# K'V of two units in four 64x64 quarters, summed in two banks that one row of matmuls claims

## The chip, the cores and the metric

One core of a Trainium2 chip runs the whole program. The metric is the device time of one execution in microseconds (us); lower is better. The kernel before takes 1583.36 us (median of three runs, 1583.11 to 1583.88).

## The reference

```python
# 8 batches, 8 heads, 576 tokens, 64 wide; q, k, v float32
kv  = np.einsum('bhsd,bhse->bhde', k, v)            # K'V: 64 x 64 for each head
out = np.einsum('bhsd,bhde->bhse', q, kv)
rms = np.sqrt(np.mean(out * out, axis=-1, keepdims=True) + 1e-06)
x   = out / rms * g_norm                            # then (4608, 512), heads side by side
h   = x @ w_in                                      # 512 -> 2048
g   = s * np.maximum(h, 0) ** 2 + b
x   = g @ w_out                                     # 2048 -> 512
h   = x @ w_in2
out = (h * np.cos(h)) @ w_out2                      # the second layer, same sizes
```

The change touches the first line alone: K'V of each head, a sum over 576 tokens.

## The kernel before

The program has two parts. The first (up to some 360 us) does attention and 48 steps of the first layer, 3 token blocks of 512 by 16 slices of the hidden width. A step has four groups of hidden-layer matmuls (`mm_h`, L877 to L879, three matmuls in each), which sum into PSUM bank h0 or h2; ScalarE (L891) and, from step 12 on, VectorE (L898) read that bank; then four groups of second-layer matmuls (`mm_o`, L926 for the first block's steps 0 to 11, in plain float32, and L930 after that), which sum into other banks (a0 to a3). The rest of the program, with the second layer, reuses weights and products in a Strassen-like scheme (L1084, L1215 and others) and is not touched.

Attention is spread over the first part. A *unit* is two heads. The first token block has its K'V from `kv_first` (L689, K and V as 9 rows on 128 partitions, one head on each half). For every later batch two units at a time are done as one *row*, one operation on TensorE: first `mm_x` (L787) multiplies q' of two units by their K'V into the halves xa and xb of banks h1 and h3, in 64x64 quarters; then `kv_pair` (L712) makes K'V of the next two units. There are 14 such rows; the first holds K'V alone. `kv_pair` reads K and V as 96 partitions by 6 rows, four tiles for two units (three slots kv_raw and the slot raw), multiplies 96x64 pieces in two column halves, 6 passes x 2 heads x 2 units = 24 matmuls, and sums both units in one bank, h0 or h2, side by side. ScalarE copies each unit's K'V to kvf (L718, 128x64, two in a row). Also in h0 or h2: four transposes a unit (L822) some us behind the row, read by ScalarE (L854 or L861) and for early blocks by VectorE (L856). GpSimd's queue (POOL, called SUM in the code) loads K and V from the third block on (L660), SP's queue before; the loads wait until the row before has read the tiles. The same POOL queue stores pieces of the first layer's weights (L614, L617).

The order of all this is not written by hand. `Plan` takes operations with an engine, a cost in us, a due time and the tiles that they read and write, plays the program on a model of the engines, and picks at each point the ready operation with the earliest due time; a search over shifted due times keeps orders in which the modelled TensorE idles least. An operation that needs PSUM banks starts, in the model, when all of them are free. `START` is when each engine is first free in the model, `AFTER` and `SLACK` are the delay behind an operation and a factor on its cost. The order found is the order on each engine; on the chip each instruction waits for its own inputs and for its own bank.

```python
    SLACK = {"PE": 1.0, "DVE": 1.14, "ACT": 1.14, "POOL": 1.0}
    AFTER = {"PE": 0.2, "DVE": 0.13, "ACT": 0.14, "POOL": 0.13}
    ACC, HB0, HB1, HB2, HB3 = slots("a", 4), ["h0"], ["h1"], ["h2"], ["h3"]
```

## Time and profile before

| | |
|---|---|
| median of three runs | 1583.36 us |
| the profiled execution | 1583.36 us, its span 1581.6 us |
| TensorE matmuls busy | 1566.9 us, 99% |
| TensorE weight loads busy | 1462.7 us, 92% |
| VectorE, ScalarE busy | 76%, 72% |
| share of the chain that ended last on TensorE | 96% |
| L712 (K'V of the rows) | 672 instructions from 69.6 to 289.3 us |

The span is what the trace covers of the profiled execution; some 1.8 us lie around it. PE is TensorE's matmuls, PEld its weight loads, which run beside matmuls, DVE is VectorE, ACT ScalarE, POOL GpSimd. A float32 matmul stands in the trace as two instructions. The start of a weight load is the sharper mark: the ends of matmuls are modelled. "Idle before" is time in which an engine stood still, with what ended it.

### The profile page before, as it was taken

How to read it: one execution, taken by the hardware profiler on the slowest of the kernel's cores; microseconds unless marked ns; L12 is line 12 of the kernel's file. 1: busy time of each engine (PE TensorE's matmuls, PEld its weight loads, DVE VectorE, ACT ScalarE, POOL GpSimd, SP SyncE). 2: the span in 40 equal slices, each digit the busy share in tenths (PEclk: the TensorE clock that was granted, in tenths of full speed). 3: DMA queues.
4: the chain of work that ended last, by engine and by line, in shares of the span. 5: the costliest groups of instructions: out<-in, count | busy, mean ns of one | idle time of the engine just before them, and what ended most of it. 6: DMA issues, size and time to landing. Idle time of an engine off the chain costs nothing.

```text
span 1581.6 us, 30681 instructions
## 1 busy us (share of the span) xinstructions
PE 1566.9 (99%) x11200; PEld 1462.7 (92%) x11200; DVE 1208.5 (76%) x2335; ACT 1142.4 (72%) x2088; POOL 54.3 (3%) x90
## 2 busy tenths in 40 slices
PE   8999999999999999999999999999999999999998
PEld 7667888888999999999999999999999999999998
DVE  5888776687667667657778888888888888888776
ACT  5875654456667767657888888887887888888773
POOL 0012322000000000000000000000000000000000
PEclk9999999999999999999999999999999999999999
DMA  9856888859889988868987888978978878978857
GB/s 322 244 121 167 243 225 223 244 175 308 305 254 296 304 263 274 304 228 293 345 251 257 298 254 263 314 252 262 306 253 263 307 252 264 308 254 259 270 186 238
DMA packets 261814, 413.09 MB, mean 261 GB/s; under 512 B 88608, under 2 KB 169504, under 8 KB 261664
## 3 DMA queue, kind: packets, MB, share of 16 engines
q1 hardware_dynamic: 255072, 389.57, 76.9%
q0 software_dynamic: 6016, 20.45, 4.7%
q8 instruction: 89, 1.46, 0.4%
q10 hardware_dynamic: 576, 1.11, 0.2%
q14 instruction: 61, 0.50, 0.1%
HBM read 327.16 MB, written 83.89 MB: 260 GB/s over the span
## 4 chain that ended last, share of the span: by engine, by line
PE 96%; DMA 2%; ACT 1%; DVE 0%; issue 0%; SPq 0%; POOL 0%; DVEq 0%; POOLq 0%
PE banks L1084 37%; PE banks L1215 22%; PE banks L978 13%; PE banks L930 6%; PE banks L1222 4%; PE banks L877 3%; PE banks L878 3%; PE banks L926 3%; PE banks L879 3%; PE banks L787 1%; PE banks L712 1%; PE banks L822 1%; DMA q_raw<-in_q_dram 1%; DMA wi<-w2n_d 1%; PE banks L1378 0%; PE banks L689 0%
## 5 line engine op out<-in xcount | busy, mean ns | idle before, releaser
L1084 PE MATMUL banks<-shared,wi 128*128 128x384 f32 x2232 | 461.7, 337 | 1.0 <-ACT g L1097 1.0
L1084 PEld LDWEIGHTS banks<-shared,wi 128*128 128x128 f32 x2232 | 389.6, 188 | 4.2 <-ACT g L1097 1.3
L1215 PE MATMUL banks<-wi,fs 128*128 128x256 f32 x2250 | 290.2, 282 | 1.5 <-DMA wi<-w2n_d 0.9
L1215 PEld LDWEIGHTS banks<-wi,fs 128*128 128x128 f32 x2250 | 284.9, 190 | 2.0 <-DMA wi<-w2n_d 1.1
L978 PE MATMUL banks<-wi,wo 128*128 128x256 f32 (+1 forms) x984 | 210.5, 337 | 0.0
L978 PEld LDWEIGHTS banks<-wi,wo 128*128 128x128 f32 x984 | 161.5, 188 | 18.4
L1097 ACT ACTIVATE t<-banks 128x384 f32<-128x384 f32 x218 | 106.6, 489 | 99.2 <-PE banks L1084 74.4
L1133 DVE TENSOR_TENSOR fs<-fu,fs 128x384 fp32r<-128x384 f32 x240 | 129.6, 555 | 25.5 <-ACT fs L1132 24.0
L1132 ACT CAST fs<-fu 128x384 fp32r<-128x384 f32 x240 | 120.1, 507 | 17.8 <-PE banks L1215 12.1
L1084 PE MATMUL banks<-late,wi 128*128 128x384 f32 x552 | 125.3, 337 | 0.1
L1084 PE MATMUL banks<-g,wi 128*128 128x384 f32 x504 | 113.0, 338 | 0.0
L930 PE MATMUL banks<-g,wo 128*128 128x512 f32 x432 | 109.3, 396 | 0.0
L1170 ACT ACTIVATE wi<-wi 128x768 f32<-128x768 f32 x96 | 80.9, 842 | 27.1 <-DVE wi L1106 26.7
L1084 PEld LDWEIGHTS banks<-late,wi 128*128 128x128 f32 x552 | 97.1, 188 | 1.1 <-DVE c L497 0.5
L1176 DVE CUSTOM_DVE_ANT_0 wi<-wi,wi 128x768 f32<-128x768 f32 x96 | 91.2, 954 | 8.3 <-ACT wi L1174 8.2
L930 PEld LDWEIGHTS banks<-g,wo 128*128 128x128 f32 x432 | 79.3, 188 | 16.1
L1084 PEld LDWEIGHTS banks<-g,wi 128*128 128x128 f32 x504 | 87.3, 188 | 0.4 <-ACT t L1097 0.3
L1215 PE MATMUL banks<-wi,raw 128*128 128x256 f32 x612 | 84.0, 282 | 1.0 <-DMA wi<-w2n_d 1.0
L877 PE MATMUL banks<-shared,wi 128*128 128x512 f32 x192 | 81.7, 426 | 1.3 <-ACT shared L854 0.8
L1215 PEld LDWEIGHTS banks<-wi,raw 128*128 128x128 f32 x612 | 80.7, 189 | 1.3 <-DMA wi<-w2n_d 1.3
L1178 ACT ACTIVATE wi<-wi 128x768 f32<-128x768 f32 x96 | 80.5, 839 | 1.0 <-DVE wi L1176 0.9
L1172 ACT ACTIVATE wi<-wi 128x768 f32<-128x768 f32 x96 | 80.5, 843 | 0.1
(194 smaller groups left out, 2740.7 us busy)
## 6 DMA issues: line engine op xcount, KB each, us to landing
wi<-w2i_d SPq DMA_DIRECT2D x144, 512.0 KB, 4.7
wi<-w1i_d SPq DMA_DIRECT2D x96, 512.0 KB, 5.2
wi<-w2s_d SPq DMA_DIRECT2D x96, 512.0 KB, 4.5
wi<-w2n_d SPq DMA_DIRECT2D x40, 512.0 KB, 3.9
wi<-w2n_d SPq DMA_DIRECT2D x64, 256.0 KB, 4.0
late<-x_d SPq DMA_DIRECT2D x36, 384.0 KB, 6.2
wi<-in_moe_w_in_dram SPq DMA_DIRECT2D x24, 512.0 KB, 8.2
w2i_d<-t SPq DMA_DIRECT2D x48, 256.0 KB, 5.2
```

Of the source, the lines that this page charges most:

```text
L877: nc.tensor.matmul(h.t, wh, hi, start=(c == 0), stop=False)
L930: nc.tensor.matmul(o.t, a[:, sl], b, start=(first and z == 0), stop=(last and z == 2))
L978: nc.tensor.matmul(dst, x[:, sl], y[:, src], start=(first and z == i == 0), stop=(last and z == 2), skip_group_check=a >= 4)
L1084: nc.tensor.matmul(o.t[:, 0:HT], a, b, start=(first and c == z == 0), stop=(c == 1 and z == 2), skip_group_check=not first)
L1097: op("ACT", 0.38, by - 40, lambda: nc.scalar.activation(dst(), o.t[:, 0:HT], func), p=[s], r=[o])
L1132: op("ACT", 0.42, by, lambda: nc.scalar.copy(x.t[:, 0], src()), w=[x], r=[ref], after=after)
L1133: op("DVE", 0.47, by + 0.4, lambda: nc.vector.tensor_tensor(out=x.t[:, 1], in0=src(), in1=f32(x.t[:, 0]), op=ALU.subtract), w=[x], r=[ref])
L1170: op("ACT", 0.75, at, lambda u=u, x=x: nc.scalar.activation(u.t, x.t, AF.Identity, scale=1.0 / TWO_PI, bias=0.25), w=[u], r=[x])
L1172: op("ACT", 0.75, at + 0.5, lambda u=u, v=v: nc.scalar.activation(v.t, u.t, AF.Identity, bias=MAGIC), w=[v], r=[u])
L1176: op("DVE", 0.88, at + 2, lambda u=u, v=v: nc.vector._custom_dve(TENSOR_ADD_SAT, out=u.t, in0=u.t, in1=v.t, s0=0.5 - 1.7e-7, s1=-0.5 + 1.7 ...
L1178: op("ACT", 0.75, at + 3, lambda u=u: nc.scalar.activation(u.t, u.t, AF.Sin, scale=TWO_PI), w=[u])
L1215: nc.tensor.matmul(dst, x.t[:, a, sl], w.t[:, at, b, :], stop=(last and z == 2), start=(first and z == 0 and (m == 0 or (m == 2 and opens) ...
```

## The change

K and V of two units are loaded as 9 rows of 64 numbers on all 128 partitions, two tiles in place of four. Each load fills one half of the partitions of one tile with two heads: the lower half gets the first head of the first unit and the second head of the second, the upper half the other two, so that the heads are crossed over the halves. There are still four loads a row. Each of the 9 passes has four matmuls of 64x64, one for each pair of a partition half and a column half: 36 matmuls in place of 24. The first unit sums in bank h0, the second in h2. The row names both banks as a claim: while it is ready within 3 us and has no banks yet, the planner holds back TensorE operations that are due later and want one of them. Besides, the costs that the planner is told of the row, of the first units' products and of the plain float32 matmuls change, and so do the times at which TensorE and ScalarE are taken to start.

```diff
-    START = {"PE": 1.4, "DVE": 1.0, "ACT": 2.9, "POOL": 4.2, "SP": 0.8, "SUM": 4.2, "AQ": 0.8}
+    START = {"PE": 2.4, "DVE": 1.0, "ACT": 3.5, "POOL": 4.2, "SP": 0.8, "SUM": 4.2, "AQ": 0.8}
+    CLAIM = 3.0
...
                 base = max(engines[e], lanes[e][0]) if e in lanes else engines[e]
+                claims = [o for o in ops if o.claim and ready_at[o.n] < base + self.CLAIM]
+                if claims:
+                    c = min(claims, key=lambda o: due[o.n])
+                    ops = [o for o in ops if o is c or due[o.n] < due[c.n] or not any(
+                        slot[i] is None and c.claim.intersection(slots) for i, slots in o.placed)]
...
-    KV_RAW, Q_RAW = [*slots("kv_raw", 3), "raw"], slots("q_raw", 2)
+    KV_RAW, Q_RAW = slots("kv_raw", 2), slots("q_raw", 2)
...
-    def kv_load(queue, t, src, b, h0):
+    def kv_load(queue, t, src, b, h0, half):
+        heads = src[b, h0 + 1:h0 + 3] if half else src[b, h0:h0 + 4:3]
         queue.dma_start(
-            out=t.t[0:KP, 0:2 * R * D].rearrange("p (h r d) -> p h r d", h=2, r=R),
-            in_=src[b, h0:h0 + 2].rearrange("h (p r) d -> p h r d", r=R))
+            out=t.t[half * D:(half + 1) * D, :].rearrange("p (g n) -> p g n", g=2),
+            in_=heads.rearrange("g (p r) d -> p g (r d)", r=R0))
...
-        ps, loaded = pref(HB2 + HB0), []
-        for hp in hps:
-            pair = [sref(KV_RAW, F32, (2 * R * D,)) for i in range(2)]
+        ps, pair = [pref(HB0), pref(HB2)], [sref([KV_RAW[i]], F32, (2 * S,)) for i in range(2)]
+        for t, src in zip(pair, (k, v)):
             eng, queue = ("SP", nc.sync) if j < 2 else ("SUM", nc.gpsimd)
-            in_turn["kv"] = [op(eng, 0.95, by - 9, lambda t=t, src=src, hp=hp: kv_load(queue, t, src, b, 2 * hp), w=[t],
-                                after=after, behind=in_turn.get("kv", ())) for t, src in zip(pair, (k, v))]
-            loaded.append(pair)
+            in_turn["kv"] = [op(eng, 0.95, by - 9, lambda t=t, src=src, half=half: kv_load(queue, t, src, b, 2 * hps[0], half),
+                                p=[t], after=after, behind=in_turn.get("kv", ())) for half in range(2)]
...
         def mm():
-            for n, (k_t, v_t) in enumerate(loaded):
-                for r in range(R):
-                    for h in range(2):
-                        nc.tensor.matmul(ps.t[h * D:(h + 1) * D, n * D:(n + 1) * D], rows(k_t, h, r), rows(v_t, h, r),
-                                         start=(r == 0), stop=(r == R - 1))
+            for r in range(R0):
+                for h in range(2):
+                    for n in range(2):
+                        half = h if n == 0 else 1 - h
+                        k_r, v_r = (t.t[half * D:(half + 1) * D, n * S + r * D:n * S + (r + 1) * D] for t in pair)
+                        nc.tensor.matmul(ps[n].t[h * D:(h + 1) * D, 0:D], k_r, v_r, start=(r == 0), stop=(r == R0 - 1))
...
         return op("PE", cost, by, lambda: [x[0]() for x in parts], w=[y for x in parts for y in x[1]],
-                  r=[y for x in parts for y in x[2]])
+                  r=[y for x in parts for y in x[2]], claim=[*HB0, *HB2])
...
-        op("PE", 0.45, by - 3, transpose_x, w=[xT], r=[xn])
+        op("PE", 0.38, by - 3, transpose_x, w=[xT], r=[xn])
...
-        x_ops.append(op("PE", 0.65, by - 8, mm, w=w, r=r))
+        x_ops.append(op("PE", 1.04, by - 8, mm, w=w, r=r))
...
-            row(0.85, by - 13, [kv[:3]])
+            row(1.25, by - 13, [kv[:3]])
...
-        x_ops.append(row(1.25 + (0.7 if kv else 0), by - 8, [*parts, kv and kv[:3]]))
+        x_ops.append(row(1.1 + (1.2 if kv else 0), by - 8, [*parts, kv and kv[:3]]))
...
-            done = op("PE", 0.87 if native else 0.69, by + step * m, lambda m=m, o=acc[m]: mm(m, o), w=[acc[m]],
+            done = op("PE", 0.91 if native else 0.69, by + step * m, lambda m=m, o=acc[m]: mm(m, o), w=[acc[m]],
...
-        op("ACT", 0.3, -99, lambda: nc.scalar.activation(
+        op("ACT", 1.4, -99, lambda: nc.scalar.activation(
```

## Rows read from the trace of the kernel before

**Rows 1.** The page: busy time of each engine, and the chain that ended last.

```profile
PE 1566.9 (99%) x11200; PEld 1462.7 (92%) x11200; DVE 1208.5 (76%) x2335; ACT 1142.4 (72%) x2088; POOL 54.3 (3%) x90
...
PE 96%; DMA 2%; ACT 1%; DVE 0%; issue 0%; SPq 0%; POOL 0%; DVEq 0%; POOLq 0%
```

**Rows 2.** Stretches: length, busy PE, PEld, DVE, ACT, POOL, granted clock, DMA share, GB/s.

```profile
0.00:20.00 20.00, 17.57 (x312) 16.52 (x314) 7.65 (x16) 8.66 (x18) 2.99 (x10) 1.00 0.85 288
20.00:40.00 20.00, 16.62 (x133) 11.92 (x129) 15.66 (x38) 13.47 (x26) 0.00 (x0) 1.00 1.07 354
...
180.00:240.00 60.00, 59.55 (x672) 49.58 (x672) 49.68 (x105) 31.33 (x66) 20.54 (x32) 1.00 0.85 227
```

**Rows 3.** Waits of TensorE's matmuls over the whole span: total us, times, longest.

```profile
PE banks L1378 <- POOL ident masks.py:199: 2.4, 1, 2.4
PE banks L1215 <- DMA wi<-w2n_d: 2.0, 2, 1.0
...
PE banks L787 <- DVE qT L771: 0.5, 1, 0.5
```

**Rows 4.** Timeline of weight loads, 87.9 to 91.0: the second row (start, us, count last).

```profile
87.91 1.02 PEld L787 LDWEIGHTS banks<-kvf,qT 64*64 64x64 f32 x64 [0.75 <-issue]
89.00 0.78 PEld L712 LDWEIGHTS banks<-kv_raw,kv_raw 96*64 96x64 f32 x24
89.69 0.79 PEld L712 LDWEIGHTS banks<-raw,kv_raw 96*64 96x64 f32 x24
90.55 0.19 PEld L877 LDWEIGHTS banks<-shared,wi 128*128 128x128 f32 x1
```

**Rows 5.** Line L712 over the span, one unit of two: count, ns, first and last start.

```profile
L712 PEld LDWEIGHTS banks<-raw,kv_raw x336: 138/138/138, 70.3 to 289.3; 96*64 96x64 f32 x168
```

**Rows 6.** Timeline of weight loads: kv_first, and what follows it on the same tile shape.

```profile
14.40 1.13 PEld L689 LDWEIGHTS banks<-wo,wo 64*64 64x64 f32 x36
15.45 1.02 PEld L747 LDWEIGHTS banks<-ident,wi 64*64 64x64 f32 x32
```

**Rows 7.** Stretches of 0.2 us: weight loads of L787, then of L712, that touch them.

```profile
88.30:88.50 0.20, 0.20 (x23) 1.00 0.00 0
...
89.30:89.50 0.20, 0.20 (x12) 1.00 0.00 0
```

**Rows 8.** Timeline of matmuls around the first row.

```profile
69.32 0.40 PE L879 MATMUL banks<-shared,wi 128*128 128x512 f32 x1
69.64 0.92 PE L712 MATMUL banks<-kv_raw,kv_raw 96*64 96x64 f32 x24
...
71.19 0.50 PE L877 MATMUL banks<-shared,wi 128*128 128x512 f32 x1
```

**Rows 9.** Timeline: the two readers of a hidden-layer sum, and what they waited for.

```profile
109.70 0.60 ACT L891 ACTIVATE t<-banks 128x512 f32<-128x512 f32 x1 [1.51 <-PE banks L879]
...
110.33 0.75 DVE L898 SCALAR_TENSOR_TENSOR t<-t,small,banks 128x512 f32<-128x512 f32 x1 [1.08 <-ACT t L891]
```

**Rows 10.** Timeline of ScalarE: copies of K'V behind the second row, the last behind the fourth.

```profile
90.67 0.33 ACT L718 COPY kvf<-banks 128x64 f32<-128x64 f32 x2 [0.44 <-PE banks L712]
...
118.41 0.21 ACT L718 COPY kvf<-banks 128x64 f32<-128x64 f32 x1
```

**Rows 11.** Last loads of two rows, their median landing, and the matmuls that use them.

```profile
92.16 0.64 POOL L660 DMA_DIRECT2D raw<-in_v_dram  x1
...
105.88 0.65 POOL L660 DMA_DIRECT2D raw<-in_v_dram  x1
...
raw<-in_v_dram POOLq DMA_DIRECT2D x12, 288.0 KB, 6.3
...
102.53 0.92 PE L712 MATMUL banks<-kv_raw,kv_raw 96*64 96x64 f32 x24
...
115.01 0.92 PE L712 MATMUL banks<-kv_raw,kv_raw 96*64 96x64 f32 x24
...
116.56 0.50 PE L877 MATMUL banks<-shared,wi 128*128 128x512 f32 x1
```

More of the change, by code (lines that the diff above doesn't have):

```diff
@@ L94, in __init__, with op @@
         self.parts = {}
-    def op(self, eng, cost, due, fn, w=(), p=(), r=(), keep=(), after=(), behind=(), lag=0.0):
+    def op(self, eng, cost, due, fn, w=(), p=(), r=(), keep=(), after=(), behind=(), lag=0.0, claim=()):
         o = Op()
+        o.claim = set(claim)
         o.eng, o.cost, o.due, o.fn, o.lag, o.refs = eng, cost, due, fn, lag, list(dict.fromkeys([*w, *p, *r, *keep]))
@@ L310, in fused_kernel @@
     NF1 = NP1 - NU
-    KP = 96
-    R = S // KP
     NQ, R0 = TB // D, S // D
@@ L408, in fused_kernel @@
     LATE = slots("late", 7)
-    EARLY = {*KV_RAW[:3], *Q_RAW, *KV_F, *QT, *AT}
+    EARLY = {*KV_RAW, *Q_RAW, *KV_F, *QT, *AT}
     RING, PLACES, X_RAW = WI[:5], slots("s", 11), LATE[:4]
@@ L695, in kv_pair @@
     def kv_pair(j, b, hps, by, after):
-        ps, loaded = pref(HB2 + HB0), []
-        for hp in hps:
-            pair = [sref(KV_RAW, F32, (2 * R * D,)) for i in range(2)]
+        ps, pair = [pref(HB0), pref(HB2)], [sref([KV_RAW[i]], F32, (2 * S,)) for i in range(2)]
+        for t, src in zip(pair, (k, v)):
             eng, queue = ("SP", nc.sync) if j < 2 else ("SUM", nc.gpsimd)
-            in_turn["kv"] = [op(eng, 0.95, by - 9, lambda t=t, src=src, hp=hp: kv_load(queue, t, src, b, 2 * hp), w=[t],
-                                after=after, behind=in_turn.get("kv", ())) for t, src in zip(pair, (k, v))]
-            loaded.append(pair)
-        def rows(t, h, r):
-            return t.t[0:KP, 0:2 * R * D].rearrange("p (h r d) -> p h r d", h=2, r=R)[:, h, r, :]
-        def mm():
-            for n, (k_t, v_t) in enumerate(loaded):
-                for r in range(R):
-                    for h in range(2):
-                        nc.tensor.matmul(ps.t[h * D:(h + 1) * D, n * D:(n + 1) * D], rows(k_t, h, r), rows(v_t, h, r),
-                                         start=(r == 0), stop=(r == R - 1))
+            in_turn["kv"] = [op(eng, 0.95, by - 9, lambda t=t, src=src, half=half: kv_load(queue, t, src, b, 2 * hps[0], half),
+                                p=[t], after=after, behind=in_turn.get("kv", ())) for half in range(2)]
+        def mm():
+            for r in range(R0):
[4 more added lines that the diff above has]
+                        nc.tensor.matmul(ps[n].t[h * D:(h + 1) * D, 0:D], k_r, v_r, start=(r == 0), stop=(r == R0 - 1))
         def copy():
@@ L717, in copy @@
                 tf = kv_f[b % 2, hp]
-                op("ACT", 0.21, by - 3, lambda n=n, tf=tf: nc.scalar.copy(tf.t, ps.t[:, n * D:(n + 1) * D]), w=[tf], r=[ps])
-        return mm, [ps], [x for pair in loaded for x in pair], copy
+                op("ACT", 0.21, by - 3, lambda n=n, tf=tf: nc.scalar.copy(tf.t, ps[n].t[:, 0:D]), w=[tf], r=[ps[n]])
+        return mm, ps, pair, copy
     xs = {}
```

## The prediction

> **What bounds the kernel now.** I began with the page. TensorE is busy for 99% of the span, and 96% of the chain that ended last is TensorE [rows 1]. A change pays only if it takes time from TensorE's own stream, and it costs if it makes TensorE wait. Next, the stretches: the rows that the change touches run from 69.6 to 289.3 us (the first and last L712 starts [rows 5, 8]). The worst of the four stretches of 60 us from 60 to 300 has TensorE busy for 59.55 of 60, VectorE for 49.68 and ScalarE for 31.33, at a granted clock of 1.00, the higher of its two levels (2.4 GHz) [rows 2]. The list of TensorE's waits agrees: in that stretch only the 0.5 us for qT is worth a name [rows 3]. So this stage is a gapless stream of matmuls, and each microsecond cut from it arrives at the end, if no gap opens.
>
> **How fast a small matmul is.** Each matmul of this kind stands in the trace as two instructions: a row of K'V has 24 in the code and 48 in the trace, 14 rows make 672, half of them on the second unit [rows 4, 5]. In kv_first, 36 weight loads on two 64x64 tiles take from 14.40 to 15.45 us, where instructions of the same tile shape follow: 18 couples in 1.05 us, 58.3 ns a couple [rows 6]. L712 (96 rows, two column halves) works in couples too: the second unit starts 0.69 us behind the first, 12 couples at 57.5 ns; all 24 are 1.40 us, and 1.55 stand there (89.00 to 90.55) [rows 4]. The 0.15 left over is the change to the shape that follows (128x128). L787, the product with q' on the four 64x64 quarters, issues 64 in 1.09 us (87.91 to 89.00): 16 sets of four at 58.3 ns are 0.93, and again some 0.15 for the change, here to 96 rows [rows 4]. The counts in flight show it too: 23 loads touch a 0.2 us window of L787, 12 one of L712 [rows 7]. So a set takes 58 ns however many tiles are in it, and four quarters do twice the work of two halves.
>
> **Part 1, the quarters.** A row now takes 9 x 2 x 2 = 36 matmuls, 72 instructions, in place of 48. On four quarters they are 18 sets: 18 x 58.3 ns = 1.05, and 0.15 for the change of shape behind them, 1.20 us against 1.55: 0.35 less, in 14 rows 4.9 us. In 13 rows (all but the first, by the code of attn_pair) L787 stands ahead, now of the same 64x64 shape, so the 0.15 between the two goes as well (as between L689 and L747 [rows 6]): 1.95 us. **Together 6.85 us** of TensorE's stream. Bounds: if the sums that stay open over nine passes, or the order (row half changes before column half), kept only two tiles in flight, the row would be 36 x 58.3 ns = 2.10 + 0.15, 0.70 longer than now. I take four in flight: L787 has the same shape, the same two row halves into two banks, and L689 keeps a sum open over nine passes at the common 58.3 ns [rows 4, 6].
>
> **Part 2, two banks claimed.** This is the cost. Before, a row sums into one of the banks h0, h2; the other could hold a hidden-layer sum, even one half done: at 69.64 us the row cuts into a run of L877 to L879, whose last three follow it, as in 7 of the 14 rows [rows 8]. Now both must be empty when the row's K'V starts, and both stay taken until ScalarE has copied them. (a) Before the row: a hidden sum is read by ScalarE from 109.70, as soon as its last matmul is done, to 110.30, and by VectorE from 110.33 to 111.08 [rows 9], so its bank is free 1.4 us later. Two things cover that: the second-layer matmuls (L926 or L930, four a step, 0.69 us each in the planner's costs), and L787 itself, 1.09 us, which uses other banks and runs ahead of K'V in the same row. I price it at nothing; uncovered it would be 1.4 - 1.09 = 0.33 us in a row, and up to 0.7 more if the reader is queued behind one other ScalarE or VectorE operation (0.60 to 0.75 [rows 9]). (b) Behind the row: the first copy starts 0.12 us after the next matmul would (90.67 against 90.55), the two end 0.33 later, at 91.00 [rows 4, 10]. A hidden-layer matmul put right behind the row would wait 0.33 to 0.45 us; second-layer matmuls put there hide it. Where ScalarE has other work first, a copy comes later (one at 118.41, 1.85 us behind the row [rows 10]), but that holds back only the one who needs that bank. The planner is told of the claim, and its model charges the copy (0.2 + 0.21 x 1.14 + 0.14 = 0.58 us), so it will mostly put second-layer work there. As the new order can't be read from this trace, I take one row in four paying 0.45: 14 / 4 x 0.45 = **1.6 us lost**. Bounds: nothing, and in each row 0.45 (6.3 us).
>
> **Part 3, loads and buffers.** Four loads a row as before, 288 KB each, 0.64 us of GpSimd each [rows 11]; POOL's w1i stores stay queued behind the same number. 128 pieces of 2304 bytes replace 192 of 1536. Buffers come free with the row's last matmul, as before. The tightest row: last load issued at 105.88, median landing 6.3 us, K'V at 115.01, so 2.8 us to spare; the one before: 92.16 + 6.3 against 102.53, 4.1 [rows 11]. Price nothing. "raw" is no longer lent to K and V; nothing else wants it in this stage. The 28 copies keep number and size.
>
> The Trainium skill (SBUF — State Buffer, "Door 1: The DMA port swizzle") speaks against the loads: a transfer to partitions 0 to 63 reaches half of the DMA ports. No transfer here has that span, so no row shows it. As a mechanism of this kernel: were a landing to take twice its 6.3 us, the two tightest rows would wait 3.5 and 2.2 us, 5.7 together: the rival "late loads".
>
> **Part 4, the planner's constants.** They issue nothing, but the search gives another order everywhere. In the first 40 us TensorE is idle for 5.8 us (17.57 and 16.62 busy of 20), 2.4 of it before the first instruction [rows 2, 3], so at most 3.4 are to be won; the largest wait of the later stages is L1215's for its weights, 2.0 us in two times [rows 3]. Truer costs may win some of it, new luck may lose as much: nothing, with 1.5 us either way.
>
> **The sum.** The profiled execution took 1583.36 us (span 1581.6 and 1.8 around it), the same as the median of the runs. 1583.36 - 6.85 + 1.6 = **1578.1 us**. Behind the row VectorE is next, at 50 of 60 us in that stretch [rows 2], which a stage shorter by 2% doesn't fill.
>
> **Rivals.** *Copies become the bound.* Every row is followed by a hidden-layer matmul that waits 0.45: 14 x 0.45 = 6.3 lost, **1582.8**, no difference. For it: hidden-layer work follows many rows now (at 71.19, 90.55 and 116.56 for three [rows 4, 8, 11]) and is due first; against it: second-layer work is there to go between. The Trainium skill (TensorEngine Tiling (Array Packing), "PSUM Bottleneck") says that after such a speed-up the copy out of PSUM may be the bottleneck. By that rule this rival holds; the trace has ScalarE idle just before the copy (0.44 us [rows 10]), so it bears the rule out only where nothing else is put in between.
> *The banks don't come empty in time, the slower side.* Where the planner finds no second-layer work ahead of the row either, a row pays 0.33 before, 0.45 behind, and up to 0.7 for a busy reader: 0.78 to 1.48, 10.9 to 20.7 us in all, **1587 to 1597, 1590** in the middle. It breaks even at 6.85 / 14 = 0.49 us a row and is measurably slower from 0.72. For it: 7 rows cut into an open sum now, which can't be any more. Against it: L787 covers 1.09 us of the drain.
> *The quarters don't do what they say:* two tiles in flight, 0.70 more a row, less 0.15 in 13: 14 x 0.70 - 13 x 0.15 = 7.9, **1591**. Against it: L787's rate.
> *Late loads:* 5.7 lost, **1583.8**.
>
> **How the numbers follow.** Forecast 0.60, 1576.6 to 1580.1 (1.5 either way, and up to a third of the rows paying); copies 0.24; banks 0.10; quarters 0.03; late loads 0.03. A difference of under 0.2% (3.2 us) can't be told from none. Faster is the forecast, 0.60; the same, copies and late loads, 0.27; slower, banks and quarters, 0.13. The range goes from all 6.85 kept with 1.4 more from the first 40 us, 1575.2, to the copies' case with 1.2 more lost, 1584.0; some 0.13 to 0.2 is left out, nearly all of it above.
>
> **What would show it.** In the changed trace: 72 weight loads a row instead of 48, from first to the next other line in 1.2 us, and 0.06 instead of 0.2 between L787's last and the first of K'V; no hidden-layer sum open across a row; TensorE still busy for all but 2 us of 60 to 300; no wait for kv_raw. A list of waits with a line of 0.3 to 0.5 us, ten times or more, of a hidden-layer matmul for the kvf copy, makes the copies' rival right; waits of the K'V line for ScalarE's or VectorE's reading of a hidden sum, the banks'. Sets of two in K'V would make Part 1 wrong, and a gap over 2 us in the first 40 or behind 360 us the nothing of Part 4.

## The result: slower, and the profile of the changed kernel

The changed kernel takes 1591.46 us (median of six runs, 1586.53 to 1595.80), the kernel before beside it 1583.23 us (six runs, 1581.17 to 1584.37): the ratio is 1.0052 with a 95% interval of 1.0029 to 1.0074, so it is slower. The forecast was 1578.1 us, at most 1584.0. The profiled execution of the changed kernel took 1587.57 us, its span 1585.8.

Line numbers shift by a few: L715 is K'V (L712 before), L789 the product with q' (L787), L879 to L881 and L928, L932 the hidden-layer and second-layer matmuls, L824 the transposes of T behind attention (L822), L773 VectorE's transposition of q (L771), L766 its loads (L764), L666 the loads of K and V (L660). In the kernels of the experiments the same lines stand up to four further down.

The page, engines and chain, after [rows 1 for before]:

```profile
PE 1562.1 (99%) x11536; PEld 1456.5 (92%) x11536; DVE 1209.2 (76%) x2335; ACT 1144.8 (72%) x2088; POOL 52.3 (3%) x90
...
PE 93%; DMA 3%; DVE 1%; ACT 1%; SPq 1%; issue 0%; DVEq 0%; ACTq 0%
```

TensorE works 4.8 us less than before (1566.9), and yet the program is longer: TensorE's share of the chain fell from 96% to 93%, and DMA, VectorE and SP's queue each have one point more of it. Where it fell is seen in the stretches (length, busy PE, PEld, DVE, ACT, POOL, clock, DMA share, GB/s) and in the list of TensorE's waits over the span, after:

```profile
60.00:120.00 60.00, 53.12 (x496) 33.79 (x495) 45.52 (x97) 39.63 (x76) 4.78 (x8) 0.91 0.75 179
120.00:180.00 60.00, 57.94 (x759) 45.90 (x758) 47.68 (x99) 35.14 (x72) 15.98 (x26) 1.00 0.73 183
180.00:240.00 60.00, 58.60 (x649) 48.34 (x648) 48.78 (x102) 31.23 (x62) 16.23 (x26) 1.00 0.85 224
```

```profile
PE banks L824 <- DVE at L817: 6.9, 1, 6.9
PE banks L1380 <- POOL ident masks.py:199: 2.4, 1, 2.4
PE banks L749 <- ACT qT L754: 1.6, 1, 1.6
PE banks L824 <- DVE shared L858: 1.4, 1, 1.4
PE banks L932 <- ACT c L949: 1.2, 1, 1.2
```

The stretch that had no gap worth a name [rows 2, 3] now has 11.1 us of gaps between 60 and 362 us (0.5 before), 6.88 of them in one place. The other gaps of the span, up to TensorE's last matmul, are 8.2 us (9.8 before).

**The one gap, followed back.** TensorE's matmuls around it, after:

```profile
106.45 0.39 PE L881 MATMUL banks<-shared,wi 128*128 128x512 f32 x1
113.71 1.01 PE L824 MATMUL banks<-ident,at 128*128 128x128 f32 x4 [6.88 <-DVE at L817]
```

VectorE in the same stretch, after:

```profile
101.57 1.28 DVE L807 TENSOR_REDUCE sm<-at 128x8 f32<-128x512 f32 x2
111.58 0.71 DVE L773 STREAM_TRANSPOSE qT<-q_raw 128x512 f32<-128x512 f32 x1 [8.72 <-DMA q_raw<-in_q_dram]
112.21 0.20 DVE L811 SCALAR_TENSOR_TENSOR sm<-sm 128x8 f32<-128x8 f32 x2
112.37 0.24 DVE L813 SCALAR_TENSOR_TENSOR sm<-sm 128x8 f32<-128x8 f32 x2
112.57 0.24 DVE L815 SCALAR_TENSOR_TENSOR sm<-sm 128x8 f32<-128x8 f32 x2
112.77 1.29 DVE L817 TENSOR_TENSOR at<-banks,sm 128x512 f32<-128x512 f32 x2
```

L773 transposes the q of the *next* unit and stands, in VectorE's queue, ahead of L811 to L817, which normalise the row just done. It waits 8.72 us for its q; the four lines behind it, which need no q, wait with it, and so do the transposes L824 and the hidden-layer work that follows them. GpSimd's and SP's queues in that time, after (SPq: what it issued from 93 to 105 us, q loads of this unit and of the next in one line):

```profile
93.45 11.73 SPq L766 DMA_DIRECT2D q_raw<-in_q_dram  x12
```

```profile
101.75 1.19 POOL L666 DMA_DIRECT2D kv_raw<-in_k_dram  x2 [14.16 <-PE banks L715]
102.96 1.19 POOL L666 DMA_DIRECT2D kv_raw<-in_v_dram  x2
```

The last four q loads of the waiting unit are issued from 102.26 to 103.76, among and behind the next row's four loads of K and V (288 KB each, issued from 101.75 to 103.55, landing at 105.5 to 110.5), and land from 105.85 to 111.20. In the planner's own timetable they were issued by 98.54 and had landed at 100.68. Before, the last one was issued at 100.08 and the K and V loads began at 103.91, so q had landed by 102.37. Over the stage VectorE stands idle for 21.9 us just before L773, in 8 times; before it was 3.5 in 3.

SP was late already when K and V came. In both kernels' traces it never issues a load before the one that it issued eight ahead of it has landed (1350 loads each; the least distance is 0.02 us). In the changed kernel the q loads at 88.14, 90.14, 93.45 and 97.81 us each come 0.02 us behind such a landing: those of four weight loads of 512 KB, issued from 82.92 to 84.47. One row earlier, K and V had been sent out right behind those weight loads, from 85.19 to 87.00 (before: 90.23 to 92.16), and the last of them took 12.1 us to land. That they slowed the weight loads is argued, not tested.

**The clock.** From 109.1 us on, in the gap, the granted clock falls to 0.50, the lower of the two levels (1.2 GHz), until 119.4. That stretch, and weight loads at either level, after:

```profile
109.12:119.36 10.24, 5.65 (x14) 3.50 (x15) 5.64 (x16) 3.16 (x5) 0.00 (x0) 0.50 0.42 57
```

```profile
118.78 0.33 PEld L880 LDWEIGHTS banks<-shared,wi 128*128 128x128 f32 x1 [0.52 <-issue]
119.22 0.27 PEld L881 LDWEIGHTS banks<-shared,wi 128*128 128x128 f32 x1
...
119.75 0.19 PEld L880 LDWEIGHTS banks<-shared,wi 128*128 128x128 f32 x1
119.98 0.19 PEld L881 LDWEIGHTS banks<-shared,wi 128*128 128x128 f32 x1
```

The step from L880 to L881 is 0.44 us at the lower level and 0.23 at the higher. At that ratio, 5.65 us of busy TensorE cost some 2.7 us more than they would have. Before, the clock stayed at 1.00 from 6 to 1579 us. The changed kernel has a second such stretch, in the first units, behind the wait of 1.6 us of L749; by the same ratio it costs 1.6 us:

```profile
13.55:16.97 3.42, 3.42 (x36) 3.08 (x36) 2.78 (x8) 1.87 (x4) 0.00 (x0) 0.50 1.05 382
```

**The account of the profiled execution** (+4.2 us): TensorE busy -4.8, gaps from 60 to 362 us +10.6, other gaps -1.6. The -4.8 are K'V and the product with q' -6.6 (each matmul from its start to the next one's, without idle time), the two stretches of the lower clock some +4.3, and the other lines -2.5, most of it in L1084 and L1215 (-1.3 and -1.2), which the change doesn't touch. The median of the six runs lies 3.9 us above the profiled one; their mean granted clocks go from 0.997 (1586.53 us) down to 0.993 (1594.37 and 1595.80). That the longer ones lose more in the same way fits this; only one was traced.

### The profile page after: what moved, and what is told of

Its sections match the earlier page's. It is cut to its first block, busy times and chain, and to the rows that moved or that the text cites. A ratio compares the mean times of both kernels' runs of the same rounds, so it can differ in the third digit from the quotient of the medians.

```text
span 1585.8 us, 31345 instructions
## 1 busy us (share of the span) xinstructions
PE 1562.1 (99%) x11536; PEld 1456.5 (92%) x11536; DVE 1209.2 (76%) x2335; ACT 1144.8 (72%) x2088; POOL 52.3 (3%) x90
## 4 chain that ended last, share of the span: by engine, by line
PE 93%; DMA 3%; DVE 1%; ACT 1%; SPq 1%; issue 0%; DVEq 0%; ACTq 0%
PE banks L1086 37%; PE banks L1217 22%; PE banks L980 12%; PE banks L932 5%; PE banks L1224 4%; PE banks L879 2%; PE banks L928 2%; PE banks L881 2%; PE banks L880 2%; PE banks L789 1%; PE banks L824 1%; DMA q_raw<-in_q_dram 1%; PE banks L715 1%; SPq L766 1%; DMA wi<-in_moe_w_in_dram 1%
## 5 line engine op out<-in xcount | busy, mean ns | idle before, releaser
L1086 PE MATMUL banks<-shared,wi 128*128 128x384 f32 x2208 | 451.0, 337 | 0.7 <-DVE wi L1106 0.6
L1086 PEld LDWEIGHTS banks<-shared,wi 128*128 128x128 f32 x2208 | 383.6, 188 | 5.5 <-DVE wi L1106 1.0
L980 PE MATMUL banks<-wi,wo 128*128 128x512 f32 (+1 forms) x1016 | 212.8, 337 | 0.0
L980 PEld LDWEIGHTS banks<-wi,wo 128*128 128x128 f32 x1016 | 165.9, 188 | 18.6
L932 PE MATMUL banks<-g,wo 128*128 128x512 f32 x432 | 111.3, 398 | 1.2 <-ACT c L949 1.2
L1086 PEld LDWEIGHTS banks<-late,wi 128*128 128x128 f32 x576 | 100.3, 188 | 0.7
L932 PEld LDWEIGHTS banks<-g,wo 128*128 128x128 f32 x432 | 78.8, 188 | 17.4 <-ACT c L949 1.6
L879 PE MATMUL banks<-shared,wi 128*128 128x512 f32 x192 | 81.3, 424 | 0.9 <-ACT t L863 0.8
```

Source lines behind the costliest of these rows:

```text
L879: nc.tensor.matmul(h.t, wh, hi, start=(c == 0), stop=False)
L932: nc.tensor.matmul(o.t, a[:, sl], b, start=(first and z == 0), stop=(last and z == 2))
L980: nc.tensor.matmul(dst, x[:, sl], y[:, src], start=(first and z == i == 0), stop=(last and z == 2), skip_group_check=a >= 4)
L1086: nc.tensor.matmul(o.t[:, 0:HT], a, b, start=(first and c == z == 0), stop=(c == 1 and z == 2), skip_group_check=not first)
```

## Experiments

Three theories stood against each other. **Theory 1**: the new order is at fault: a load that lands late holds VectorE's queue, TensorE runs dry, the clock falls. **Theory 2**: the claim on two banks costs this in any order. **Theory 3**: the shorter row is at fault; TensorE gets ahead of what feeds it, and a row that ends earlier also frees K's and V's tiles earlier, so that their loads go out ahead of the q loads. (Later texts say in their own words what they mean by a theory.) Each ratio is to the kernel before in the same session, and is taken over all runs.

In the table "profiled" is the time of the profiled execution, and the columns behind the ratio are read from it: "q waits" is VectorE's idle time just before its transpositions of q, "gaps" TensorE's idle time from 60 to 362 us, "busy" TensorE's busy time. Runs of one kernel with quarters or pairs on two banks can spread widely (9 us for the changed kernel, 14 for seed2_a, against 3 to 4 for the kernel before), and the profiled one can lie far from the median. So 3 us between two such medians show little.

| kernel | median us | profiled | ratio to before [95%] | q waits | gaps | busy |
|---|---|---|---|---|---|---|
| before | 1582 to 1583 | 1583.36 |  | 3.5 | 0.5 | 1566.9 |
| e3_constants | 1581.94 | 1581.80 | 1.0004 [0.9995, 1.0014] | 1.1 | 0.0 | 1566.9 |
| seed3_b | 1585.26 | 1584.51 | 1.0020 [1.0011, 1.0030] | 6.6 | 1.8 | 1567.5 |
| seed5_b | 1582.52 | 1582.21 | 1.0000 [0.9991, 1.0009] | 2.7 | 0.9 | 1567.4 |
| f1_before_late6 | 1589.53 | 1589.81 | 1.0041 [1.0026, 1.0056] | 0 | 0.1 | 1570.7 |
| after | 1591.46 | 1587.57 | 1.0052 [1.0029, 1.0074] | 21.9 | 11.1 | 1562.1 |
| seed2_a | 1590.22 | 1599.14 | 1.0061 [1.0038, 1.0083] | 15.9 | 14.9 | 1567.3 |
| seed3_a | 1583.29 | 1584.51 | 1.0001 [0.9990, 1.0012] | 13.1 | 5.4 | 1561.2 |
| e1_moved | 1583.91 | 1584.47 | 1.0014 [0.9998, 1.0029] | 19.2 | 7.7 | 1561.6 |
| e8_kv_behind | 1583.61 | 1587.02 | 1.0011 [1.0000, 1.0022] | 15.4 | 8.8 | 1562.9 |
| e9_mixed | 1589.35 | 1584.04 | 1.0039 [1.0028, 1.0051] | 14.9 | 6.6 | 1562.8 |
| e2_pairs | 1587.98 | 1586.19 | 1.0046 [1.0030, 1.0062] | 9.8 | 2.0 | 1569.1 |
| e5_no_claim | 1601.20 | 1600.95 | 1.0120 [1.0103, 1.0137] | 10.7 | 7.6 | 1567.5 |
| e11_late4 | 1583.93 | 1583.85 | 1.0008 [0.9999, 1.0018] | 2.7 | 1.4 | 1562.9 |
| e11_late6 | 1577.84 | 1578.45 | 0.9966 [0.9953, 0.9979] | 0 | 5.0 | 1559.0 |
| f3_seed3_late6 | 1584.15 | 1581.27 | 1.0009 [0.9999, 1.0019] | 0 | 4.3 | 1561.8 |
| f3_seed2_late6 | 1585.54 | 1589.29 | 1.0022 [1.0006, 1.0037] | 1.4 | 5.8 | 1564.4 |
| f2_pairs_late6 | 1585.20 | 1584.03 | 1.0014 [1.0004, 1.0023] | 0 | 0.8 | 1570.3 |

### Is it that one wait? e1_moved and e8_kv_behind

e1 keeps the order of the changed kernel but for one operation: the sixth transposition of q is put behind eight normalising ones.

```diff
         s = self.search()
+        at = [i for i, o in enumerate(s.order) if o.eng == "DVE" and "q_later" in o.fn.__qualname__]
+        for i in reversed(at[5:6]):
+            norm = [n for n, o in enumerate(s.order) if n > i and o.eng == "DVE" and "normalised" in o.fn.__qualname__]
+            s.order.insert(norm[7], s.order.pop(i))
```

> The order that the planner found for the changed kernel, with one instruction moved: the sixth transposition of q on VectorE (the one that stood still for 8.7 us for its loads in the changed kernel) goes behind the eight normalising operations that it stood ahead of. Theory 1 (the loss is the new order: a VectorE queue held by a late q load, then the lower clock): the gap of 6.9 us at 107 us and the half clock behind it go, 7 to 10 us less than the changed kernel, 1578 to 1581 us. Theory 2 (the loss is the claim on two banks): nothing of that gap moves away by more than 1 us, since the banks are as before; 1586 or more.

e8 keeps every engine's order and issues the four K and V loads of the third row from SP's queue, behind the q loads.

```diff
             eng, queue = ("SP", nc.sync) if j < 2 else ("SUM", nc.gpsimd)
+            if j == 2 and hps[0]:
+                queue = nc.sync
```

> The changed kernel with the planner's order unchanged, and only the four loads of K and V behind the third row (101.75 to 103.55 us in the changed kernel) issued from SP's queue, where they stand behind the loads of q that VectorE's sixth transposition waits for, in place of POOL's. If those loads of q are late because K and V got into the DMA queues ahead of them, the last of them lands by 106 us instead of 111.2, the transposition waits under 2 us instead of 8.7, the gap of 6.9 us shrinks to under 1, and the time falls by 6 to 10 us to 1579 to 1583. If they are late for another reason (SP's own waits), the gap stays above 5 us and the time within 2 us.

e1 took 1583.91 us, 7.6 less than the changed kernel, and e8 1583.61, 7.9 less; both lie above the ranges that were expected if the loads are the cause. The same transposition in e8 (VectorE's timeline):

```profile
106.50 0.71 DVE L775 STREAM_TRANSPOSE qT<-q_raw 128x512 f32<-128x512 f32 x1 [1.41 <-DMA q_raw<-in_q_dram]
```

Its last q load goes out at 104.18 us there, later than in the changed kernel (103.76), and lands 1.95 us later, in place of 7.44; TensorE has no gap of 0.2 us or more between 60 and 150 us. In e1 the transposition still waits for its q, and L862, which makes the input of the next hidden-layer group, now stands behind it, so that 2.28 of the 6.88 us are left. VectorE and TensorE in e1:

```profile
109.52 0.71 DVE L777 STREAM_TRANSPOSE qT<-q_raw 128x512 f32<-128x512 f32 x1 [4.65 <-issue]
111.58 0.50 PE L883 MATMUL banks<-shared,wi 128*128 128x512 f32 x1 [2.28 <-DVE shared L862]
```

(The page names no load before this transposition; the last of its q loads landed at 109.24.) Both edits leave arithmetic and TensorE's order as they were; e8 takes the gap away and e1 two thirds of it. So that gap, with the clock behind it, came from a q load that was overtaken by K and V and from an order that let it hold VectorE's queue: that much of Theory 1, and of Theory 3 the loads' part, is shown. What it cost in all is less sure: the medians fall by 7.6 and 7.9 us, but the profiled executions only by 3.1 and 0.6, and neither median gets below the kernel before, for other gaps came up. e8's waits of TensorE from 60 to 362 us:

```profile
PE banks L826 <- DVE shared L860: 3.2, 1, 3.2
PE banks L881 <- ACT t L865: 2.3, 1, 2.3
PE banks L826 <- DVE t L902: 1.9, 2, 1.0
PE banks L934 <- ACT c L951: 1.5, 1, 1.5
```

### Slower rows in the same order: e2_pairs and e9_mixed

e2 keeps the order and makes one unit's K'V after the other's, so that two quarters are in flight; e9 does so for 3 of the 9 passes.

```diff
-            for r in range(R0):
-                for h in range(2):
-                    for n in range(2):
+            for n in range(2):
+                for r in range(R0):
+                    for h in range(2):
```

```diff
+            pairs = [(r, h, n) for n in range(2) for r in range(3) for h in range(2)]
+            quarters = [(r, h, n) for r in range(3, R0) for h in range(2) for n in range(2)]
+            for r, h, n in pairs + quarters:
```

> The changed kernel with the loop over the two units outermost in K'V, so that only two of the four quarters are at work at a time; the order on all engines is the same. If a set costs 58 ns whatever is in it, a row's K'V takes 36 sets, 2.25 us instead of 1.24, 14 us more of TensorE time in 14 rows. If TensorE's stream bounds this stage, 9 to 14 us more at the end (some may fall into the gap at 107 us, which a load ends); if the loads bound it, under 4 us more.

> The changed kernel, order unchanged, with three of the nine passes done two quarters at a time and six done four at a time: 24 sets, the TensorE time that a row's K'V took in the kernel before, 1.55 us, so 4.7 us more TensorE time than in the changed kernel; both banks claimed as in the change. Theory 3 (the gaps come from the speed: a shorter row asks for its loads earlier and starts its own K and V loads earlier, ahead of loads of q): the gaps from 60 to 360 us shrink to 2 to 5 us, and the time stays within 3 us of the changed kernel or falls below it. Theory 2 (the claim): gaps of 8 us or more as in the changed kernel, and 3 to 5 us more time.

In pairs a row's K'V takes 2.09 us, 0.85 more than with quarters (the 14.7 us of the expectation were too much: 14 x 0.85 = 11.9). Yet e2 took 1587.98 us, no more than the changed kernel (the intervals of the two ratios overlap): its gaps are 2.0 us for 11.1 and its clock doesn't fall. Its stretch from 60 to 120 us:

```profile
60.00:120.00 60.00, 60.00 (x644) 40.22 (x643) 51.50 (x108) 43.39 (x85) 4.78 (x8) 1.00 0.71 172
```

So in this order the gain of the quarters is lost in full: TensorE waits for what it now reaches sooner. The last q load went out at 102.50 there, before the K and V loads at 103.64, as Theory 3 has it. e9 was to have rows as long as before, but a row with its product takes 2.32 us there, for 2.16 in the changed kernel and 2.64 before. It is between (1589.35 us, 6.6 us of gaps), outside of both expectations for the gaps.

### Constants and orders without the claim: e3_constants, seed3_b, seed5_b

e3 is the kernel before with the new START and costs alone; seed3_b and seed5_b are the kernel before with another seed of the planner's search (the diff shows seed 3).

```diff
-    START = {"PE": 1.4, "DVE": 1.0, "ACT": 2.9, "POOL": 4.2, "SP": 0.8, "SUM": 4.2, "AQ": 0.8}
+    START = {"PE": 2.4, "DVE": 1.0, "ACT": 3.5, "POOL": 4.2, "SP": 0.8, "SUM": 4.2, "AQ": 0.8}
...
-        op("ACT", 0.3, -99, lambda: nc.scalar.activation(
+        op("ACT", 1.4, -99, lambda: nc.scalar.activation(
```

```diff
-        rnd = random.Random(1)
+        rnd = random.Random(3)
```

> The kernel before, with K'V as it was (96 rows, one bank, no claim), and of the change only the planner's constants: when TensorE and ScalarE are taken to start, the costs of the first warm-up on ScalarE, of the first units' products, of the transposes and of the plain float32 matmuls. Priced at nothing, with 1.5 us either way: 1580.4 to 1583.4. If truer costs win the first 40 us, 1 to 3 us less; if any new order loses what the tuned one had, 2 to 8 us more, with gaps between 60 and 360 us that the kernel before hasn't.

> The kernel before with seed 3 for the planner's random due times; the model gives 9.94 us of idle TensorE against 11.03 for the kernel before. If its lack of gaps from 60 to 360 us (0.54 us) is the luck of one order, this order has gaps of 3 us or more there and 1583 to 1590 us. If one bank a row lets any order run without gaps, under 1.5 us of gaps and 1580 to 1584 us.

> The kernel before with seed 5; the model gives 8.99 us of idle TensorE. The same expectations as for the kernel before with seed 3: gaps of 3 us or more from 60 to 360 us if the order is what counts, under 1.5 us if one bank a row is.

1581.94, 1585.26 and 1582.52 us, gaps of 0 to 1.8 us: the constants alone cost nothing, and with the kernel before four orders of the old kind lie within some 3.3 us of each other. (seed3_b lies a little outside of both its expectations.) A fifth, f1 below, does not.

### Other orders of the changed kernel: seed2_a, seed3_a, e5_no_claim

The changed kernel with seeds 2 and 3 (the diff shows 2), and with its claim emptied (seed 1).

```diff
-        rnd = random.Random(1)
+        rnd = random.Random(2)
```

```diff
-                  r=[y for x in parts for y in x[2]], claim=[*HB0, *HB2])
+                  r=[y for x in parts for y in x[2]], claim=())
```

> The changed kernel with another seed (2) for the planner's random due times; its model gives 8.65 us of idle TensorE instead of 8.73. Theory 1 (the loss is the luck of one order): the gaps from 60 to 300 us lie elsewhere and have another sum, anything from 2 to 15 us, and the time lies between 1576 and 1592. Theory 2 (the claim costs it in any order): gaps of 8 to 12 us again, 1586 to 1592.

> The changed kernel with seed 3; the model gives 8.62 us of idle TensorE. The same expectations as for seed 2: by theory 1 the gaps from 60 to 300 us differ in place and sum from both other orders; by theory 2 they come to 8 to 12 us again.

> The changed kernel without the claim in the planner: a row still needs both banks, but nothing is held back for it. The model's idle TensorE is 23.1 us instead of 8.7. If the model is right on what TensorE waits for by itself, 12 to 16 us more than the changed kernel, 1600 or more; if the chip's gaps are those of loads alone, within 4 us of it.

1590.22 and 1583.29 us: three orders of the new kind spread over 8 us, with gaps of 5.4 to 14.9 us, neither of the new two in Theory 2's 8 to 12. The gaps aren't at the same places (the first two waits of seed2_a, over the span):

```profile
PE banks L824 <- DVE t L900: 5.8, 2, 4.6
PE banks L879 <- DVE t L900: 4.6, 1, 4.6
```

Without the claim it is worse, 1601.20 us: a row starts, for the planner, when both banks are free at once, and now nothing keeps others from taking one of them first. The last row's K'V starts at 362.4 us instead of 295.9, in the middle of the next stage's matmuls. TensorE in e5:

```profile
378.57 1.16 PE L789 MATMUL banks<-kvf,qT 64*64 64x64 f32 x64 [0.36 <-DVE at L817]
379.66 0.66 PE L824 MATMUL banks<-ident,at 128*128 128x128 f32 x4
383.31 1.32 PE L1086 MATMUL banks<-shared,wi 128*128 128x384 f32 x6 [2.99 <-DVE wi L1106]
```

So the claim as a rule of the planner helps, by 10 us here, in one order each. That two banks needed together make orders harder to find is argued from this; in that sense Theory 2 isn't refuted. The old K'V with two banks claimed was not run, which would tell the banks from the faster row.

### A margin for the loads: e11_late4, e11_late6, f3_seed3_late6, f3_seed2_late6, f1_before_late6

The planner alone is told that the q loads of later batches are seen 4 (6) us after its model of the DMA lands them. f3 has the margin of 6 with seeds 3 and 2, f1 the same margin in the kernel before.

```diff
-                end = seen = s.dma + self.LANDS + o.lag
+                end = s.dma + self.LANDS + o.lag
+                seen = end + o.late
...
-                           behind=in_turn.get("q", ())) for seg in segments(j) for z in range(4)]
+                           behind=in_turn.get("q", ()), late=6.0) for seg in segments(j) for z in range(4)]
```

> The changed kernel, with one number more for the planner: what waits for a load of q is taken to see it 4 us later than the model of the DMA queues says. The model's idle TensorE is 8.9 us, as before. If the loss is in loads that come later than planned and block VectorE's queue, the waits of the transpositions fall under 5 us in all (22 us in the changed kernel), the gaps from 60 to 360 us under 4 us, and the time to 1576 to 1580 us, 2 to 6 under the kernel before. If the claim costs it in any order, 8 us or more of gaps and 1584 to 1592.

> The same with 6 us; the model's idle TensorE is 8.5 us. The same expectations: 1576 to 1580 us if late loads of q are the cause; 1584 to 1592 if the claim is.

> The kernel before (two column halves, one bank, old constants), with one edit: its planner is told that the q loads of the later batches are seen 6 us after its model of the DMA lands them. Theory 1 (the order of the changed kernel had no margin for a late q load; the old order had it already, with waits for q_raw of 3.5 us in all and gaps of 0.54 us between 60 and 360 us): nothing to win, 1582 to 1585, and up to 1589 if the planner's own idle time, 17.4 us in its model against 11.0, is to be believed. Rival (the margin itself makes a kernel faster, and the quarters had no part in the 1577.84 of the changed kernel with margin): 1577 to 1579 here.

> The changed kernel with the margin of 6 us and another seed of the planner's search (3 for 1): another order. Theory 1 (the margin is what was missing): 1576 to 1580; the planner's model idles as long as with seed 1 (9.0 us against 8.5). Rival (the 1577.84 was one lucky order among claimed orders that spread from 1583 to 1591): anywhere from 1581 to 1591.

> The same with seed 2, which without the margin took 1590.22. The planner's model idles 14.1 us here, 5.6 more than with seed 1. Theory 1: the large gaps between 60 and 360 us (14.85 us without the margin) fall under 6 us, time 1577.8 to 1584 (5.6 more if the planner's own idle time arrives). Rival (luck, or the claim costs in any order): gaps over 8 us, 1585 to 1591.

With 6 us the changed kernel took **1577.84 us** (1575.90 to 1578.45), 0.34% less than the kernel before, and faster than both. The wait for q is gone, and the stretch that had lost 6.88 us is full. e11_late6, its first stretch and its waits from 60 to 362 us:

```profile
60.00:120.00 60.00, 60.00 (x657) 39.05 (x656) 53.62 (x116) 44.82 (x87) 8.56 (x14) 1.00 0.75 182
```

```profile
PE banks L825 <- DVE sm L814: 2.3, 1, 2.3
PE banks L825 <- DVE t L901: 1.7, 1, 1.7
PE banks L716 <- DVE t L901: 1.0, 1, 1.0
```

(The last row is the claim itself: a row that waited 1.0 us for a bank that VectorE still read.) But the two other seeds hold Theory 1 down. The margin of 6 us takes the waits for q to 0, 1.4 and 0 us in the orders of seeds 1, 2 and 3 (from 21.9, 15.9 and 13.1), and the gaps to 5.0, 5.8 and 4.3 us; in time seed 2 wins 4.7 us (1585.54) and seed 3 nothing (1584.15). Both times lie outside Theory 1's range and where the rival had them, by which 1577.84 is one lucky order. e11_late4, at 1583.93 us and so outside its range too, has few gaps in this stage but 6.9 us of them behind it. The mean of the three orders with the margin, 1582.5 us, is that of the kernel before, and 5.8 below the mean without. What is left is TensorE waiting for VectorE, mostly for banks that it reads; f3_seed2_late6:

```profile
PE banks L825 <- DVE t L901: 4.7, 2, 3.6
PE banks L790 <- DVE qT L774: 0.7, 1, 0.7
PE banks L933 <- DVE g L915: 0.3, 1, 0.3
```

In the kernel before the margin brings nothing: 1589.53 us, about the upper end of Theory 1. There was next to no gap to close in the stage, and its new order loses in the later stages (8.3 us of gaps there against 4.0) and in TensorE's busy time (3.8 us more). So the margin by itself made no kernel faster. Why one order of the quarters reaches 1577.84 us isn't shown: f3_seed3_late6 has the same idle time of TensorE over the span (17.6 us, for 17.7) and takes 6.3 us more by the median, 2.8 by the profiled execution.

### The worth of the quarters where the margin is: f2_pairs_late6

e11_late6 with K'V in pairs, as e2.

```diff
-            for r in range(R0):
-                for h in range(2):
-                    for n in range(2):
+            for n in range(2):
+                for r in range(R0):
+                    for h in range(2):
```

> The changed kernel with the margin of 6 us, order kept to the instruction, but K'V of one unit after the other, so that two quarters are in flight: 36 sets a row in place of 18, 18 x 58.3 ns = 1.05 us more in each of 14 rows, 14.7 us more of TensorE's stream. Theory 1 (with the margin TensorE's stream sets the time again): 1577.84 + 14.7 = 1592.5, less what of the 5 us of gaps between 60 and 360 us the longer rows fill, so 1588 to 1593. Rival (as without the margin, where the same edit cost nothing, the time is set by the other engines and loads): 1577 to 1581.

1585.20 us, 7.4 more than e11_late6, where the same edit had cost nothing without the margin. The row and what follows it, in the timeline of weight loads (86.50 to 88.59, 2.09 us):

```profile
86.50 2.02 PEld L716 LDWEIGHTS banks<-kv_raw,kv_raw 64*64 64x64 f32 x72
88.59 0.31 PEld L929 LDWEIGHTS banks<-g,wo 128*128 128x128 f32 x2
```

TensorE's busy time rises by 11.3 us, its gaps fall by 4.2 in the stage and by 1.6 elsewhere: 5.6 of the 11.3 arrive in the profiled executions (1578.45 and 1584.03). The expected 1588 to 1593 was too high, by the price of the pairs (11.9, not 14.7) and by these gaps.

## Why the prediction was wrong, step by step

**How fast a small matmul is, and Part 1: right.** The second row of the changed kernel, weight loads (start, us, count last) [rows 4 for before]:

```profile
82.62 1.02 PEld L789 LDWEIGHTS banks<-kvf,qT 64*64 64x64 f32 x64 [0.75 <-issue]
83.55 1.17 PEld L715 LDWEIGHTS banks<-kv_raw,kv_raw 64*64 64x64 f32 x72
84.78 0.31 PEld L928 LDWEIGHTS banks<-g,wo 128*128 128x128 f32 x2
```

L789 now takes 0.93 us (1.09 before), and the 72 loads of L715 1.24 to the next line (1.55): a row with its product 2.16 us for 2.64, 0.48 less, and 0.34 less in the first row. 13 x 0.48 + 0.34 = 6.5 us, where 6.85 were worked out. "The quarters don't do what they say" is out. A set of two, though, is a little quicker than a set of four: without the 0.20 us from the last load to the next line's first, 36 sets in pairs take 1.89 us, 52 ns each, and 18 sets of four 1.04, 58 ns each. (Two sums of the prediction are off in the last digit: 1.4 - 1.09 is 0.31, and 1583.36 - 6.85 - 1.4 is 1575.1. Nothing hangs on them.)

**Part 2, the claim: the waits that it prices are not there.** In the changed kernel no hidden-layer matmul behind a row waits for the copy of K'V, and no row waits for its banks: the list of waits has no L715. The planner put second-layer work behind all 14 rows, as L928 above. (Other orders have such a wait once: 0.3 us for a copy in seed3_a, 1.0 and 0.3 us of a row for its banks in e11_late6 and f3_seed3_late6.) So the 1.6 us were not paid, and both "copies become the bound" and "banks don't come empty" name waits that aren't there; the second rival's time, 1587 to 1597, was met, but not by its mechanism. The Trainium skill (TensorEngine Tiling (Array Packing), "PSUM Bottleneck") says that the copy out of PSUM may become the bottleneck; in this trace it did not, with no wait for a copy of K'V in 14 rows. The price of two banks, if it is one, is paid by the order: in new orders T's transposes wait for a bank that VectorE reads (0.9 us in the changed kernel, 5.8 in seed2_a, 1.7 in e11_late6), which the list of before doesn't have, nor those of the other four orders of the old kind. That it is the claim that does this is argued, not shown.

**Part 3, loads: the right question asked of the wrong load.** K and V land much as worked out: in the changed kernel 6.7 to 8.2 us from the last issue on GpSimd's queue, in the middle 7.1 for 6.3 before [rows 11], but for the row whose loads went out right behind the weights (12.1); and no row waits for them. The Trainium skill (SBUF — State Buffer, "Door 1: The DMA port swizzle") speaks of half the ports for partitions 0 to 63; a landing twice as long would be 12.6 us, and eleven of twelve rows, whose loads each fill one half, don't show it. The rival "late loads" is out for K and V. But "price nothing" left out who else uses the DMA queues: a row that ends earlier sends its successor's 1.2 MB out earlier, and in the third row they went ahead of q. The last of those loads landed 10.5 us behind the planner's timetable.

**Part 4, a new order priced at nothing, 1.5 us either way: the step that failed.** The bound was taken from the idle time of the first 40 us and from one wait of a later stage. The stage in between had no gaps [rows 2, 3], and that was read as nothing to lose; it had 300 us of TensorE's time to lose from. In its place stood 10.6 us more of gaps there and some 2.7 us for the clock behind the largest, more than the 6.5 us that the quarters save. The constants alone were priced rightly (e3: 1581.94 us); what had no price is the order that the planner finds for shorter rows with two banks. Old orders with the planner's timetable as it was spread by not much more than was given (1581.94 to 1585.26), but f1's took 1589.53: an order alone can cost 7 us, without quarters or a second bank. New ones spread from 1583.29 to 1591.46 without a margin and from 1577.84 to 1585.54 with one. The sign named in the prediction, "TensorE still busy for all but 2 us of 60 to 300", was the one that fell: 11 us.

**The sum.** Nor did each microsecond cut from TensorE arrive. In one order none of the 11.9 us between pairs and quarters did, in another 7.4. "VectorE is next, at 50 of 60 us, which a stage shorter by 2% doesn't fill" took an engine's mean share for its slack. VectorE is never full in the changed kernel (46 to 49 of 60 in its stretches above); it is held for 8.72 us by one operation at the head of its queue.

**What stays open.** Why the orders with margin differ by 7.7 us between seeds isn't settled: their gaps differ by 1.5 us in the stage and by up to 4.5 elsewhere, and the rest lies in TensorE's busy time (1559.0 to 1564.4), in part the clock's. Nor is it told apart how much of the new orders' gaps is due to two banks and how much to the faster row; the pairs show that the row's speed has a share of 4 to 9 us of gaps, in the two orders where it was slowed.

## What to carry to other kernels

A gain on an engine that is 99% busy is worth what the queues behind it let through: list the operations that stand at the head of another engine's in-order queue waiting for a load, and ask which loads the faster stage will now send ahead of that one. Where an edit changes an order that a planner makes, take the spread of its orders as the range, from a few seeds, and not the idle time of the order at hand. A planner's model of landing times may want a margin before its orders are tightened, but the margin's worth has to be read from several orders: here 6 us turned a loss of 0.5% into a gain of 0.3% in one order, and into no difference in the mean of three.

## What the runs showed of the hardware

A gap can cost more than its length: from 2.3 us into the one of 6.88 us the granted clock was 0.50 for 10.2 us, and a step of 0.23 us took 0.44. Shorter gaps did so too in some kernels: in e1_moved, after one of 2.35 us at 219.7, it was 0.50 from 222.9 to 226.4. Four 64x64 quarters in flight are nearly twice as quick as two, but not quite: with the change of shape behind them, 72 weight loads stood in 1.24 us with four and in 2.09 in pairs. A small load can be overtaken by large ones of another queue: the four q loads issued among and behind those of K and V landed 3.6 to 7.7 us after their issue, and in e8, where K and V came behind them, the last took 1.95 us. And in this program SP's queue has at most eight loads open: of 1350 in the changed kernel none is issued before the one eight ahead of it has landed, so that four slow loads hold up all that stand behind them.
